# Loading the last 64 tokens of two batches in another order, and other transfer times for the planner of a sliding-window attention and two-matrix kernel

## The chip, the cores and the metric

The kernel runs on one core of a Trainium2 chip. The metric is the device time of one execution in microseconds (us).

## The reference

Attention with a window over 8 batches, 8 heads, 576 tokens and 64 numbers a head, then two matrix products with a leaky rectifier between them. Heads 0 to 3 see the last 32 tokens; heads 4 to 7 see every fourth of the last 128 ("dilated").

```
rel = pos[:, None] - pos[None, :]
mask_plain = (rel >= 0) & (rel < 32)
mask_dil = (rel >= 0) & (rel < 128) & (rel % 4 == 0)
attn = softmax(where(mask, q @ k.T / 8, -1e9))      # for each batch and head
x = (attn @ v), as [4608 tokens, 512]
h = x @ w_in                                        # [512, 2048]
out = max(0.01 * h, h) @ w_out                      # [2048, 512]
```

Inputs and output are float32. The kernel casts to float16 for TensorE.

## The kernel before

**Stages.** Batches 0 and 1 are "early" (`EARLY`): they are loaded in large runs of 1024 bytes (four tokens of a head), and q and k are turned by PE transposes through PSUM. Batches 2 to 7 are loaded in 128-byte pieces and turned by DVE. Each early batch is treated in two parts. Part 0 is its first 512 tokens, loaded by `load_group` in two groups of heads: group 1 (dilated) and group 0 (plain), each with q, k and v. Part 1 is "the rest", the last 64 tokens of all heads, loaded by `load_rest`: one load of q, one of k (128 KB each), one of v of the dilated heads (64 KB), and for batch 0 one of v of the plain heads (64 KB). `load_rest` casts q and k together on POOL (1024 numbers a partition), and the v loads in pieces of 512; for batch 0 it also runs a permutation of plain v on PE (`permute`).

`turn` brings q and k into the slots that the scores read. For part 1 it transposes the cast rest in eight PE transposes into the bank `tpb` and moves the result into `slots` by DVE copies (`move`, line 644). `unit` then does, for a pair of heads and a third of the tokens: scores on PE (line 854, for small dilated units 840, with a bias by line 837), the exponential on ACT (860), values and sums on PE (898, 892, 886), logarithm and exponential on ACT (930, 932), and the norm on DVE into `xt` (936). `xt` is the input of the up products.

The 4608 tokens are twelve chunks of 384 tokens, three for each pair of batches: chunk 0 is the first 384 tokens of batch 0, chunk 1 those of batch 1, chunk 2 the remaining tokens of both. `up` multiplies a chunk with a block of w_in (line 1091), and ACT applies the rectifier (1102). An up product needs all four row blocks of w_in, and all norms of its chunk. `down` (1275) and, later, `group` (1364) multiply with w_out. The last three chunks use `up_fast` (1188). w_in and w_out come in eight loads of 512 KB each (`load_w`), and each is cast to float16 in two pieces on POOL or DVE (line 272).

**The order of the work** is made by a planner, `_Plan.run`, when the kernel is built. Each task has an engine, an estimated duration, its dependencies and a priority (a lower number goes first). The planner simulates the engines and writes each engine's instructions in the order of their simulated starts; the chip runs each queue in that order, and waits are put in from the data's dependencies. A DMA is simulated as one server after another: its service is `took(n, size)` for n packets of `size` bytes, `AHEAD` says how many us of service may be queued when SP issues the next one, and `LATE` (or 0.8, or 0) us are added to the landing by the load's place. So these constants change no instruction, only the orders. From `LOCK` (60 us) on, the planner also lets POOL and DVE wait for each other on certain operations.

The first loads go in the order of the string `FIRST`, one letter a step, each with the next priority. Before, `b` and `c` are q and k of batches 0 and 1 (the first time for the dilated group, the second for the plain one), `v` and `y` their v, `i` a load of w_in, `o` a load of w_out, and `0` and `1` the rest of batches 0 and 1. `CON` places a load of constants among them. `RANKS` gives the priorities of the early batches' parts: batch 0 part 0 begins at 10 with steps of 6, its part 1 at 10 with steps of 0.5.

Where the plan leaves PE idle, a matmul on zeros is put in (line 1595). It has no use but to keep PE at work, and it waits for nothing.

Of the kernel before, what the change touches and what calls it, by code (L numbers as in the profile page):

```python
# [12 lines left out]
ALU = mybir.AluOpType  # L13

WIN = 32
AHEAD, LATE = 5.0, 4.0
WHEN = (-5.0, 15.0, 46.0, 70.0, 100.0, 126.0, 160.0, 188.0)
CON = -1484.5
LOCK = 60.0
AFTER = -1495.0  # L20
FIRST = "bvbviiii0iiiicoocoyoooooy1"
RANKS = ((10.0, 6.0), (10.0, 0.5), (15.0, 2.0), (25.0, 2.0))


# [37 lines left out]
class _Plan:  # L62
# [21 lines left out]

    def run(self):
        free, waiting, lock = {}, {}, {}
        server = 0.0

        def enter(t):
            for eng, _ in t.choices:  # L90
                waiting.setdefault(eng, []).append(t)

        for t in self.tasks:
            for d in t.deps:
                d.users.append(t)
            t.left = len(t.deps)
            if t.left == 0:
                enter(t)
        order = []
        while len(order) < len(self.tasks):  # L100
            best = None
            for eng, cand in waiting.items():
                if not cand:
                    continue
                here = free.get(eng, 0.0)
                if eng == "SP":
                    here = max(here, server - AHEAD)
                could = [t for t in cand
                         if not self.better_elsewhere(t, eng, max(here, t.ready), free)]
                if not could:  # L110
                    continue
                at = max(here, min(t.ready for t in could))
                pick = min(((t.ready + t.soft > at + 1e-9, t.prio, t.n), t)
                           for t in could if t.ready <= at + 1e-9)
                if best is None or (at, pick[1].n) < best[:2]:
                    best = (at, pick[1].n, eng, pick[1])
            at, _, eng, t = best
            for e, _ in t.choices:
                waiting[e].remove(t)
            t.eng, t.start, t.dur = eng, at, dict(t.choices)[eng]  # L120
            if at > LOCK and eng == "POOL" and t.kind in ("cast", "M", "A", "move") or (
                    at > LOCK and eng == "DVE" and t.kind in ("M", "A", "T")):
                t.dur += max(0.0, lock.get("DVE" if eng == "POOL" else "POOL", 0.0) - at)
                lock[eng] = at + t.dur
            free[eng] = at + t.dur
            if t.service:
                begin = max(at + t.dur + 0.9, server)
                server = begin + t.service
                t.done = server + 1.1 + t.late
            else:  # L130
                t.done = at + t.dur + t.lat
            order.append(t)
            for u in t.users:
                u.ready = max(u.ready, t.done)
                u.left -= 1
                if u.left == 0:
                    enter(u)
        order.sort(key=lambda t: (t.start, t.n))
        return order
# [3 lines left out]
def kernel(  # L143
# [14 lines left out]
    B, H, S, D = q.shape  # L158
# [31 lines left out]
    def dram(t, off, *dims):  # L190
        return bass.AP(tensor=t.tensor, offset=t.offset + off, ap=[list(d) for d in dims])
# [58 lines left out]


    def took(n, size):
        for a, ta, b, tb in ((4, 9.0, 128, 15.0), (128, 15.0, 256, 19.0), (256, 19.0, 1024, 48.0),
                             (1024, 48.0, 2048, 85.0)):
            if size <= b:
                return n * (ta + (tb - ta) * (size - a) / (b - a)) / 16e3
        return n * size / 25.6 / 16e3

    def load(queue, dst, src, n, size, deps, prio, slow=1.0):
        eng = ENG[queue]  # L260
        return plan.dma(queue, 0.7 if size == 128 else 0.48, took(n, size) * slow, deps,
                        lambda e: eng.dma_start(dst, src), prio,
                        LATE if prio > -1500 + len(FIRST) else 0.8 if prio >= AFTER else 0.0)

    def cast(dst, src, n, deps, prio, engines=("POOL",)):
        cost = {"POOL": 0.05 + n * 0.00102, "DVE": 0.08 + n * 0.00056, "ACT": 0.06 + n * 0.00087}
# [234 lines left out]
    def load_rest(b, prio):  # L501


        _, r_old = ring("REST", 1, r_users := [])
        sn, s_old = ring("STG", NST, s_users := [])
        st, lo = stg[sn], []
        for o, src in ((0, q), (1, k)):
            lo.append(load("SP", at(st, 0, 128, o * 256, [1, 256]),
                           dram(src, b * H * HS + 512 * D, [HS, 8], [4 * D, 16], [1, 256]),
                           128, 1024, s_old, prio))  # L510
        c = cast(at(rest, 0, 128, 0, [128, 8], [D, 2], [1, D]),
                 at(st, 0, 128, 0, [D, 8], [0, 2], [1, D]), 1024, lo + r_old, prio)
        s_users.append(c)
        vs, v_old, v_users = v_late[b]
        spread = bass.AP(tensor=vs.tensor, offset=vs.offset + 1024,
                         ap=[[4 * vs.ap[0][0], 16], [256, 4], [1, 256]])
        lv = load("SP", spread,
                  dram(v, (b * H + 4) * HS + 512 * D, [4 * D, 16], [HS, 4], [1, 256]),
                  64, 1024, v_old + t_vr[:1], prio)
        last = []  # L520
        if b == 0:
            vz, z_old, z_users = v_late[b, 0]
            lz = load("SP", bass.AP(tensor=vz.tensor, offset=vz.offset + 1024,
                                    ap=[[4 * vz.ap[0][0], 16], [256, 4], [1, 256]]),
                      dram(v, 512 * D, [4 * D, 16], [HS, 4], [1, 256]), 64, 1024, z_old + t_vr[1:],
                      prio)
            c_z = [cast(turned[i][0:64, 0:512], vz[0:64, 1024 + 512 * i:1536 + 512 * i], 512, [lz],
                        prio + 20) for i in range(2)]
            z_users += c_z
            last = permute((4, 5), c_z, RANKS[1][0], True)  # L530
            done = [t for t, _ in permuted]
            for t in t_gap:
                t.deps.extend(done)
            rings["X"] = [done, done]
        for vi in (2, 3, 0, 1):
            vt, d_users = kept[b, vi]
            c_v = []
            if vi >= 2:
                c_v = [cast(at(vt, 0, 64, 0, [1024, 2], [128, 4], [1, D]),
                            at(vs, 0, 64, 1024 + (vi - 2) * 512, [256, 2], [D, 4], [1, D]), 512,  # L540
                            [lv] + d_users, prio + 30)]
                v_users += c_v
            c_v += last[vi:vi + 1] if vi < 2 else []
            visits[b, vi, 1] = rest, [c], r_users, vt, c_v + seen_ones[b, vi], d_users
# [3 lines left out]
    def load_w(n, prio):  # L548
# [10 lines left out]
        else:  # L559
            x = 1024 * (n - 8)  # L560
            src = dram(moe_w_out, 128 * x, [2 * DM, 128], [1, 1024])
            dst = w_out
        t = load("SP", st, src, 128, 4096, old, prio, 1.3 if n < 4 else 1.0)
        for i in range(2):
            c = cast(dst[:, x + 512 * i:x + 512 * i + 512], st[:, 512 * i:512 * i + 512], 512, [t],
                     29 if n < 2 else prio, ("POOL",) if 4 <= n < 8 else CENG)
# [91 lines left out]
    def turn(b, hp, part, prio):  # L658
# [59 lines left out]
        if part == 1:  # L718
# [8 lines left out]
            if two == 2 and hp % 2:  # L727
                new = pair_moves[b, hp ^ 1]
            else:
                new, busy = [], users + other[1] * (two == 2)  # L730
                for hh, h in enumerate(heads_of(b, hp)):
                    p0 = 64 * hh
                    for o, bk in ((0, qb), (1, kb)):
                        x, dims = 512 * o + 16 * h, [[128, 4], [1, 16]]
                        if dil:
                            c, to = (0, [[144, 4], [4, 16]]) if o else (hh * S + 128, [[144, 4], [1, 16]])
                        elif o:
                            c, to, dims = PAD + 512, [[4, 16], [1, 4]], [[1, 16], [128, 4]]
                        else:
                            c, to = hh * S + 488, [[24, 4], [1, 16]]  # L740
                        step = PAD + S if o else 2 * S
                        new.append(move(at(bk, p0, p0 + 64, c, [step, two], *to),
                                        at(tpb, p0, p0 + 64, x, [32, two], *dims), 64 * two,
                                        [tq] + zq + zk + (busy if dil and o else []), prio))
                pair_moves[b, hp] = new
            q_users += new
# [752 lines left out]
    for n, step in enumerate(FIRST):  # L1499
        seen = FIRST[:n].count(step)  # L1500
        if step in "io":
            load_w(seen + (8 if step == "o" else 0), tick())
        elif step in "bvcy":
            ranks["bvcy".index(step) // 2, 1 - seen, step in "vy"] = tick()
        else:
            ranks[int(step)] = tick()

# [145 lines left out]
```

## Time and profile before

| | us |
|---|---|
| median of 3 runs (lowest, highest) | 306.11 (305.94, 306.44) |
| profiled execution, device time | 306.29 |
| its span, first to last instruction | 304.5 |
| PE busy in the span | 294.4 |
| DVE, ACT, POOL busy | 231.0, 188.7, 132.3 |

The granted clock was 1.00. A line of the profile is named L with the line of the code. A wait is put down to the instruction or the load that ended last before it. PE's busy time contains the idle matmuls (L1489 at the start, L1595 later), and a matmul's end is modelled, so that a matmul that starts 0.16 us after another may be shown 0.3 us long. The 40 slices of the span are 7.61 us each. SP is the queue that issues nearly all loads and stores; its rows show when a load is issued and not when it lands. The DMA engines moved 51.09 MB, and in the first 44 us they were busy nearly all the time.

### The profile page before, as it was taken

The numbers are of one execution on the slowest core, as the hardware profiler recorded it, in microseconds if no ns is written. First come the engines' busy times: TensorE is split into PE (matmuls) and PEld (weight loads), VectorE is DVE, ScalarE is ACT, GpSimd is POOL, SyncE is SP. The second block draws the span as 40 slices with busy tenths as digits, with TensorE's granted clock in tenths as the row PEclk, the third lists the DMA queues.
The fourth block names the chain that finished last, engine by engine and source line by source line (L and its number), as shares of the span: only waits on it lengthen the run. The fifth ranks groups of instructions, "written<-read, shape, count | busy, mean of one in ns | idle before, by whom it ended". The sixth has DMA issues, their size and how long they took to land.

```text
span 304.5 us, 7869 instructions
## 1 busy us (share of the span) xinstructions
PE 294.4 (97%) x2970; PEld 225.4 (74%) x2970; DVE 231.0 (76%) x478; ACT 188.7 (62%) x458; POOL 132.3 (43%) x179
## 2 busy tenths in 40 slices
PE   6889999999999999997999999999999999999994
PEld 3646655667777676786777777887788999999984
DVE  6875875689686869959888779879775899697552
ACT  3857854795556678464766567456565688767230
POOL 5469555393674949159094668665000000000000
PEclk9999999999999999999999999999999999999999
DMA  7999999999999899976999969793102110031124
GB/s 241 404 370 392 407 289 201 239 201 167 253 171 196 190 188 196 174 180 134 183 161 221 204 136 194 159 208 80 37 2 72 34 37 2 11 91 32 32 76 146
DMA packets 160390, 51.09 MB, mean 168 GB/s; under 512 B 137632, under 2 KB 157024, under 8 KB 160352
## 3 DMA queue, kind: packets, MB, share of 16 engines
q1 hardware_dynamic: 159520, 49.86, 68.3%
q10 hardware_dynamic: 832, 0.73, 0.8%
q8 instruction: 23, 0.38, 0.5%
q14 instruction: 15, 0.12, 0.1%
HBM read 41.13 MB, written 9.44 MB: 166 GB/s over the span
## 4 chain that ended last, share of the span: by engine, by line
PE 90%; DVE 5%; ACT 3%; DMA 1%; issue 1%; DVEq 0%
PE hps L1091 29%; PE fps L1364 26%; PE fps L1275 9%; PE ops L1015 3%; PE hps L1188 3%; PE ops L1188 3%; PE ops L1063 2%; PE sps L1188 2%; PE tp L1188 1%; PE tp L692 1%; PE ops L1364 1%; PE tp L982 1%; PE sps L982 1%; DVE ee L1008 1%; PE fps L347 1%; PE tp L975 1%
## 5 line engine op out<-in xcount | busy, mean ns | idle before, releaser
L1091 PE MATMUL hps<-xt,w_in 128*128 128x384 f16 (+1 forms) x640 | 111.7, 310 | 0.8 <-DVE w_in L272 0.6
L1102 ACT ACTIVATE gt<-hps 128x384 f16<-128x384 f32 (+1 forms) x160 | 72.8, 461 | 43.8 <-PE hps L1091 41.5
L1091 PEld LDWEIGHTS <-w_in 128*128 128x128 f16 x640 | 56.7, 98 | 26.3 <-DVE w_in L272 1.0
L1364 PEld LDWEIGHTS <-gt 128*128 128x128 f16 x672 | 64.4, 98 | 9.7
L679 POOL COPY slots<-turned 64x576 f16<-64x576 f16 x48 | 36.3, 757 | 47.4 <-DVE turned L674 45.5
L1364 PE MATMUL fps<-w_out,gt 128*128 128x256 f16 x416 | 53.6, 273 | 0.0
L272 POOL CAST nat<-stg 128x576 f16<-128x576 f32 (+1 forms) x53 | 43.0, 834 | 9.7 <-DMA stg<-in_q_dram 3.5
L1275 PE MATMUL fps<-w_out,gt 128*128 128x512 f16 x128 | 32.4, 379 | 0.0
L1037 DVE TENSOR_TENSOR rc<-ops,recs 96x384 f16<-96x384 f32 x48 | 25.7, 538 | 0.3
L1393 ACT COPY stg<-fps 128x512 f32<-128x512 f32 (+1 forms) x24 | 12.8, 532 | 14.4 <-PE fps L1364 14.4
L1008 DVE TENSOR_TENSOR ee<-ee,con 128x576 f16<-128x576 f16 x24 | 17.2, 722 | 3.5 <-ACT ee L994 3.5
L1033 DVE RECIPROCAL recs<-ops 96x6 f32<-96x6 f32 x48 | 8.7, 181 | 14.7 <-PE ops L1015 12.5
L1401 DVE TENSOR_TENSOR osb<-fps,stg 128x512 f32<-128x512 f32 x18 | 12.4, 687 | 9.7 <-PE fps L1364 5.6
L272 POOL CAST vd<-v_all 128x1024 f16<-128x1024 f32 (+2 forms) x20 | 18.0, 918 | 2.7 <-DMA v_all<-in_v_dram 2.7
L1211 ACT ACTIVATE gt<-stg 128x384 f16<-128x384 f32 x36 | 18.0, 524 | 1.1 <-DVE stg L1205 1.1
L1275 PEld LDWEIGHTS <-gt 128*128 128x128 f16 x128 | 11.6, 98 | 9.1
L644 DVE COPY slots<-tp 64x128 f16<-64x128 f16 (+7 forms) x42 | 13.4, 333 | 6.3 <-PE tp L692 5.6
L674 DVE STREAM_TRANSPOSE turned<-nat 128x576 f16<-128x576 f16 x24 | 17.7, 751 | 0.0
L685 DVE STREAM_TRANSPOSE slots<-nat 128x576 f16<-128x576 f16 x24 | 17.7, 745 | 0.0
L1008 DVE TENSOR_TENSOR el<-el,con 128x576 f16<-128x576 f16 x24 | 15.0, 630 | 2.7 <-ACT el L994 2.5
L1188 PEld LDWEIGHTS <-w_in 128*128 128x128 f16 x192 | 16.4, 98 | 0.5 <-DVE w_in L1119 0.3
L994 ACT ACTIVATE ee<-sps 128x288 f16<-128x288 f32 x24 | 9.8, 409 | 8.4 <-PE sps L982 5.8
(158 smaller groups left out, 529.3 us busy)
## 6 DMA issues: line engine op xcount, KB each, us to landing
stg<-in_q_dram SPq DMA_DIRECT2D x48, 144.0 KB, 3.2
stg<-in_k_dram SPq DMA_DIRECT2D x48, 144.0 KB, 2.9
v_all<-in_v_dram SPq DMA_DIRECT2D x24, 256.0 KB, 3.8
v_all<-in_v_dram SPq DMA_DIRECT2D x24, 192.0 KB, 3.2
gt<-in_moe_w_in_dram SPq DMA_DIRECT2D x5, 512.0 KB, 7.1
out_dram<-osb SPq DMA_DIRECT2D x22, 96.0 KB, 2.0
out_dram<-osb SPq DMA_DIRECT2D x40, 48.0 KB, 1.8
out_dram<-osb SPq DMA_DIRECT2D x25, 64.0 KB, 2.2
```

What stands on the lines that cost most here:

```text
L272: ENG[e].tensor_copy(out=dst, in_=src)
L674: lambda e: nc.vector.transpose(xb, na[:, 0:S]), prio)
L679: lambda e, p0=p0, hh=hh: nc.gpsimd.tensor_copy(out=at(qb, p0, p0 + 64, hh * S + o, *od), in_=at(xb, p0, p0 + 64, i, *id_)), prio, 0.0, "m ...
L685: lambda e: nc.vector.transpose(kb[:, PAD:PAD + S], na[:, S:2 * S]), prio)
L1008: nc.vector.tensor_tensor(out=x, in0=x, in1=mk, op=ALU.mult)
L1037: nc.vector.tensor_tensor(out=at(xb, 0, 96, 768 * n + 64 * i, [256, 3], [128, 2], [1, D]), in0=at(ot, 0, 96, 0, [130, 3], [65, 2], [1, D]) ...
L1091: nc.tensor.matmul(ht[:, 0:n], at(w_in, 0, 128, i * DFF + j // 2 * 256 + j % 2, [2, 128]), at(xt[m % 2], 0, 128, i * 1152 + x0, *dims), st ...
L1102: lambda e: nc.scalar.activation(out=gt[c % NG][:, j * n_c + x:j * n_c + x + n], in_=ht[:, 0:n], func=AF.Prelu, alpha=0.01),
L1188: nc.tensor.matmul(cell[:, n * z:n * z + n], lhs(2 * p + z, i), rhs(i), start=first and z == 0 and i == 0, stop=z == 1 and i == 1, skip_gr ...
L1211: lambda e: nc.scalar.activation(out=at(g, 0, 128, j * n_c + n * y, [n_c, 2], [1, n]), in_=at(src, 0, 128, 0, [n, 2], [1, n]), func=AF.Pre ...
L1275: nc.tensor.matmul(ft, g[:, j * n_c + tt * 128:j * n_c + tt * 128 + 128], w_out[:, j * DM:j * DM + DM], start=(j == 0), stop=(j == NJ - 1))
L1364: nc.tensor.matmul(bk[:, x:x + HN], tl[:, off + j * step:off + j * step + 128], rhs(j), start=first and x == 0 and j == 0, stop=j == HJ - ...
```

## The change

1. In `load_rest`, the source of the rest's q and k is read with the 16 groups of four tokens outermost and the 8 heads inside, instead of the heads outermost. A partition of the stage holds 8 x group + head instead of 16 x head + group. In `turn`, the eight moves of the rest read the transposed bank in steps of 8 elements instead of 1.
2. `FIRST` gets a table, `LOADS`, which gives each letter its batch, group and kind. In the string, `0` goes from behind the fourth load of w_in to before the first. The rest of the order is the same under new letters.
3. The planner counts at most eight transfers in flight for SP (`FLIGHT`) up to 60 us, `LATE` goes from 4.0 to 2.5 and the first loads' 0.8 to 0.3, `took` gets other figures for packets of 128 to 2048 bytes, and the factor of 1.3 on the first four loads of w_in goes.

```diff
-AHEAD, LATE = 5.0, 4.0
+AHEAD, LATE = 5.0, 2.5
...
+FLIGHT = 8
 AFTER = -1495.0
-FIRST = "bvbviiii0iiiicoocoyoooooy1"
+FIRST = "bvaw0iiiiiiiicooeoyooooox1"
+LOADS = {"b": (0, 1, False), "v": (0, 1, True), "a": (0, 0, False), "w": (0, 0, True),
+         "c": (1, 1, False), "y": (1, 1, True), "e": (1, 0, False), "x": (1, 0, True)}
...
-        server = 0.0
+        server, lands = 0.0, [0.0] * FLIGHT
...
                 if eng == "SP":
-                    here = max(here, server - AHEAD)
+                    here = max(here, server - AHEAD, lands[-FLIGHT] if here < LOCK else 0.0)
...
                 t.done = server + 1.1 + t.late
+                lands.append(server + 1.1)
...
-        for a, ta, b, tb in ((4, 9.0, 128, 15.0), (128, 15.0, 256, 19.0), (256, 19.0, 1024, 48.0),
-                             (1024, 48.0, 2048, 85.0)):
+        for a, ta, b, tb in ((4, 9.0, 128, 13.3), (128, 13.3, 256, 18.3), (256, 18.3, 1024, 48.5),
+                             (1024, 48.5, 2048, 95.0)):
...
-                        LATE if prio > -1500 + len(FIRST) else 0.8 if prio >= AFTER else 0.0)
+                        LATE if prio > -1500 + len(FIRST) else 0.3 if prio >= AFTER else 0.0)
...
-                           dram(src, b * H * HS + 512 * D, [HS, 8], [4 * D, 16], [1, 256]),
+                           dram(src, b * H * HS + 512 * D, [4 * D, 16], [HS, 8], [1, 256]),
...
-        t = load("SP", st, src, 128, 4096, old, prio, 1.3 if n < 4 else 1.0)
+        t = load("SP", st, src, 128, 4096, old, prio)
...
-                        x, dims = 512 * o + 16 * h, [[128, 4], [1, 16]]
+                        x, dims = 512 * o + h, [[128, 4], [8, 16]]
...
-                            c, to, dims = PAD + 512, [[4, 16], [1, 4]], [[1, 16], [128, 4]]
+                            c, to, dims = PAD + 512, [[4, 16], [1, 4]], [[8, 16], [128, 4]]
...
-                                        at(tpb, p0, p0 + 64, x, [32, two], *dims), 64 * two,
+                                        at(tpb, p0, p0 + 64, x, [2, two], *dims), 64 * two,
...
-        elif step in "bvcy":
-            ranks["bvcy".index(step) // 2, 1 - seen, step in "vy"] = tick()
+        elif step in LOADS:
+            ranks[LOADS[step]] = tick()
```

## The prediction

> **What bounds the kernel now.** I read the busy table and its forty slices first, then PE's waits, then PE's timeline where it waits, then SP's issues and the DMA rate by window, last POOL's waits and DVE's timeline in the middle. The profiled execution took 306.29 us, of which 304.5 us is the span and 1.79 us lies around it; the median of the runs is 306.11 us, 0.18 us less. All sums below are made on 306.29 and brought to the median at the end. A difference of 0.2% (0.61 us) is about the least that a measurement of this kernel can tell from none.
>
> ```profile
> PE 294.4 (97%) x2970; PEld 225.4 (74%) x2970; DVE 231.0 (76%) x478; ACT 188.7 (62%) x458; POOL 132.3 (43%) x179
> PE   6889999999999999997999999999999999999994
> ```
>
> PE is the bound. Its row is at 9 from the fourth slice (22.8 us) on, but for one 7 at 137 to 145 us and the end. So only the first 22 us and that one dip hold anything to gain. PE's waits in the whole trace, longest first (line, what it waited for, us in total, times, longest):
>
> ```profile
> PE ops L1015 <- DVE ee L1008: 1.6, 1, 1.6
> ...
> PE hps L1091 <- DVE w_in L272: 0.6, 1, 0.6
> ```
>
> The dip is one wait of 1.6 us. The early waits are short, because the program fills planned waits with idle matmuls (L1595). They count as busy, so the timeline has to be read by line (start, length, engine and line):
>
> ```profile
> 16.82 0.61 PE L1595 MATMUL fps<-warm 128*128 128x512 f16 x2
> 17.71 0.28 PE L898 MATMUL ops<-ee,vp 128*64 128x96 f16 x4 [0.29 <-DVE xt L936]
> 17.80 0.28 PE L886 MATMUL ops<-ee,ones 128*64 128x192 f16 x2
> 18.00 1.25 PE L1595 MATMUL fps<-warm 128*128 128x512 f16 x5
> 19.09 1.16 PE L1091 MATMUL hps<-xt,w_in 128*128 128x384 f16 x6
> 20.89 0.50 PE L1091 MATMUL hps<-xt,w_in 128*128 128x384 f16 x2 [0.64 <-DVE w_in L272]
> 21.22 0.38 PE L1595 MATMUL fps<-warm 128*128 128x512 f16 x1
> 21.80 1.46 PE L1091 MATMUL hps<-xt,w_in 128*128 128x384 f16 x8 [0.20 <-ACT gt L1102]
> ```
>
> From 16.82 to 21.80 us, 4.98 us, PE does eight up matmuls (1.30 us, as the eight from 21.80 to 23.10 show) and one group of values (0.29 us, 17.71 to 18.00). **The hole is 4.98 - 1.30 - 0.29 = 3.39 us.** It is bounded by the last norms of batch 0's first part (DVE, to 19.2 us) and by the fourth w_in block: it landed at 18.90 us, and its cast on DVE (19.67, 1.16 us where the same cast took 0.41 elsewhere) ended at 20.83.
>
> The loads, by window (length, clock, DMA busy share, GB/s), and then SP's issues (start, length of issuing):
>
> ```profile
> 14.00:16.00 2.00, 1.00 1.01 414
> 16.00:17.00 1.00, 1.00 1.04 344
> 17.00:18.00 1.00, 1.00 1.12 290
> 18.00:19.00 1.00, 1.00 1.06 325
> ```
>
> ```profile
> 9.46 0.79 SPq L262 DMA_DIRECT2D stg<-in_q_dram  x1
> ...
> 13.45 2.88 SPq L262 DMA_DIRECT2D gt<-in_moe_w_in_dram  x3
> 18.92 0.33 SPq L262 DMA_DIRECT2D xt<-in_moe_w_in_dram  x1
> ```
>
> The DMA engines are full, yet the rate falls while the rest of batch 0 (the loads issued at 9.46 to 12.8) passes. SP issues with eight loads in flight: the w_in load of 13.45 goes out when the load eight before it has landed (13.43), that of 18.92 after the landing at 18.90.
>
> **The change, part by part.**
>
> *Token groups outermost.* Each of the rest's q and k loads shows eight engines' completions in the trace (q 17.55 to 18.07, k 18.50 to 19.04), a w_in load sixteen; of the next w_in load eight engines finish at 18.99 to 19.66 and eight at 20.18 to 20.55. So half of the engines carried both loads: 2 x 128 packets over 8 is 32 packets of 46 ns (the row's own 1024-byte packets), 1.47 us; over 16 it would be 0.74 us. The windows agree: 3 x 414 - (344 + 290 + 325) = 283 KB lost, 0.68 us. Loads behind it come 0.7 us sooner. PE has no wait for a load from 22 to 54 us, so alone this is worth nothing there; it is what lets PE run ahead. The Trainium skill ("DMA: Bandwidth & Descriptors", how many engines, in the section on why a DMA increments its semaphore by 16) says that a DMA uses the largest count up to 16 that divides the slowest dimension of both sides, which gives 8 for 8 heads and 16 for 16 token groups; by it the spread is sure, by the rows alone it is likely. The second such load (batch 1, landed by 46.7, used at 51.20) gains as much and is waited for by nobody.
>
> *The stride of the eight moves.* They read PSUM in steps of 8 elements where they read runs. The rows have 216 to 228 ns for runs (425 to 449 where held) and 272 to 289 for those with a step of 128: at most 0.06 us x 6, 0.36 us of DVE per batch, at least nothing. I take 0.2, on DVE alone.
>
> *The rest ahead of w_in.* Four issues (0.79 + 0.62 + 0.61 + 0.57 = 2.6 us of SP) go before eight. The first w_in issue moves from 6.38 to about 9.4 us; the batch's own loads keep the engines busy until 12.17, which hides it. The 384 KB put w_in back by 384/414 = 0.93 us: the fourth block, 1.28 us behind the third (15.99), would land at 15.99 + 1.28 + 0.93 = 18.2. In the trace one engine ran 1.25 us behind the fifteen others there (17.65 to 18.90; a 16 KB instruction packet of 1.04 us lies at 16 us), so 18.2 to 19.4, against 18.90. The rest would have landed by about 13.2 instead of 19.5.
>
> On POOL the rest's cast (1.04 us) and two of 0.80 and 0.61 go between w_in casts; POOL has gaps of 0.65 to 1.84 us there. On DVE eight moves (2.07 us at 23.75) come in front of the last norms and casts. They need the transpose bank, whose last users end at 15.6, so they run at about 16.5 to 18.6. DVE is idle for 5.00 - 4.35 = 0.65 us in 17 to 22 and 0.37 in 13 to 17, so norms and casts could slip by up to 1.05 us; w_in casts going to POOL instead (0.61 each) can make it nothing. The cast held to 1.16 us stood against the rest's cast on POOL (19.51 to 20.55); that goes, worth up to 0.75 us, and can recur earlier. Ups began in effect at 21.22 - 1.30 = 19.92; I expect 19.3 to 20.9 and take +0.2 us. A rule speaks against this move: the Trainium skill ("SBUF — State Buffer", who interferes with whom) lets DVE and GpSimd block each other for a whole instruction on a shared port pair. By it the 0.75 us is moved, not saved, and the sum would be 0.75 us longer; the 1.16 us cast agrees with it.
>
> What fills the hole: the rest's PE work now lies behind it. Eight transposes 0.45 (23.10 to 23.55); four score groups 0.34 + 0.33 + 0.34 + 0.34; four value groups 0.33 + 0.33 + 0.29 + 0.29; permutations 1.52 (26.48 to 28.00): 4.56 us for a hole of 3.39. Least: the transposes, 0.45. Most: 3.39. Each unit runs scores, exponential, values, so transposes, two or three score groups and a pair of value groups are likely: 0.45 + 1.0 + 0.4, about **1.8 us taken out of PE's later path**.
>
> *Is 1.8 us kept?* At 53.77 the down products of chunk 0 are used up and chunk 1 needs the last norm of batch 1 (DVE, 53.69). Its last v landed at 44.87, was cast by 46.44, and its values ran at 48.29 to 51.75 between downs. Those downs moved forward leave the units nearer to each other; some 2 us of slack, enough for 1.8.
>
> *Planner's figures (transfer times, eight in flight, 2.5 for 4.0 us of lateness).* No instruction is added; the orders of all queues are made anew. With 1.5 us less margin a cast can stand at the head of POOL before its load. POOL's waits from 60 to 210 us, and a line of DVE's timeline:
>
> ```profile
> POOL slots L679 <- DVE turned L674: 45.5, 14, 7.3
> POOL nat L272 <- DMA stg<-in_k_dram: 2.4, 2, 2.0
> POOL nat L272 <- DMA stg<-in_q_dram: 1.1, 1, 1.1
> ```
>
> ```profile
> 139.54 2.95 DVE L1008 TENSOR_TENSOR ee<-ee,con 128x576 f16<-128x576 f16 x1
> ```
>
> POOL waits 3.8 us for loads (0.3 in a row not shown) and 45.5 for DVE: room enough, and none of the four waits for loads reached PE. The one stall that did is the mask of 139.54, held for 2.95 us (0.40 free) beside a row of POOL casts. A new order can drop it (-1.6), keep it, or make more (+1.6 each). I take +0.3, since the order before shows so few.
>
> **Sum:** 306.29 - 1.8 + 0.2 + 0.3 = 305.0 us, less 0.18: **304.8 us**.
>
> **Rivals.**
>
> *More of it:* the hole is filled to the brim (-3.39) and the 1.6 us stall goes: 306.1 - 5.0 = 301.1; half of it 302.8. For it: 4.56 us of work is at hand. Against: the chain within a unit. 0.16.
>
> *Given back at 54 us:* the units of batch 1 keep their place and PE waits there: 306.1. For: its v comes only 0.7 us sooner. Against: values 2 us behind their cast. 0.10.
>
> *Still eight engines:* w_in and all behind come 0.7 us later than I say; half shows: 305.2. Nothing in the rows speaks for it. 0.07.
>
> *Slower:* the new order between 60 and 200 us sets POOL's casts against DVE's masks more often, with PE's values queued behind, 1.6 us each as at 139.54. One more is 306.4, within the measure; it decides from two more on: 304.8 + 3.2 = 308.0. For: some twenty DVE and POOL instructions there run over 0.5 us longer than the shortest of their line and shape, and only one stall of over a microsecond comes of them, which an arbitrary new order may not repeat. Against: the planner models this lock. 0.23.
>
> **Numbers.** Forecast 0.44, 303.6 to 305.4. Faster 0.44 + 0.16 + 0.06 = 0.66, same 0.11, slower 0.23. The range takes half of the first rival and the slower case with one to two stalls: 302.6 to 307.3.
>
> **What would show it.** Right: L1595 rows after 16 us gone or few, rest transposes on PE before 18 us, sixteen completions of the rest loads, no rate below 380 GB/s from 16 to 19 us, ups in full from about 20 us. Wrong: PE waits for DVE or w_in before 22 us as long as now, a PE wait at 50 to 54 us for batch 1, or more than one wait of over 1 us after 60 us.

## The result and the profile after

The changed kernel takes **313.3 us** (median of 4 runs, 312.3 to 314.0) against 306.1 us beside it: ratio 1.0231, 95% interval 1.0210 to 1.0252. It is slower by 7.2 us; the forecast of 304.8 and the whole range, to 307.3, lie below it. Measured again (e1) it took 311.2 us, ratio 1.0159 (1.0142 to 1.0176). The two intervals don't meet; what differs is told at e1. A few runs lie more than 1.5% above the fastest of their kernel: the ratios leave them out, some medians do not, so the ratios are what I go by.

The profiled execution took 314.0 us, its span 312.2 us. The busy table and PE's row of forty slices (7.8 us each):

```profile
PE 296.9 (95%) x2963; PEld 226.4 (73%) x2963; DVE 230.7 (74%) x478; ACT 188.7 (60%) x459; POOL 128.5 (41%) x178
...
PE   6889999999999989999996999989999999999995
```

The row of before had one weak slice after 23 us. Here there are three: the fifteenth (109 to 117 us), the twenty-second (164 to 172) and the twenty-seventh (203 to 211). PE's waits in the whole trace of after, longest first (lines stand four further down than before, so L1019 is the values line that was L1015):

```profile
PE ops L1019 <- DVE ee L1012: 3.4, 3, 1.3
PE tp L696 <- POOL nat L276: 2.3, 1, 2.3
PE sps L979 <- POOL slots L683: 2.1, 1, 2.1
```

PE waits for masks (DVE) three times, for a copy by POOL once, and once, at 5.9 us, for POOL's cast of a first load. POOL's and DVE's waits from 60 to 210 us, the window that the prediction showed:

```profile
POOL nat L276 <- DMA stg<-in_q_dram: 19.7, 7, 8.8
POOL slots L683 <- DVE turned L678: 19.4, 11, 3.5
POOL nat L276 <- DMA stg<-in_k_dram: 9.0, 3, 3.1
POOL nat L276 <- DMA v_all<-in_v_dram: 2.3, 1, 2.3
```

```profile
DVE slots L689 <- POOL nat L276: 6.1, 2, 3.1
DVE turned L678 <- POOL nat L276: 0.6, 1, 0.6
```

Before, POOL waited 3.8 us for loads there, and DVE not once for POOL. Now POOL waits over 30 us for loads, and DVE 6.7 us for POOL. The casts stand at the head of POOL before their data.

To see where PE loses time I use one sum for all kernels: the time elapsed less the columns that PE's useful matmuls have streamed by then (2.4 columns a nanosecond, the 0.16 us from start to start of 384 columns). Idle matmuls count as lost, and so does half of every stretch in which PE works at half its clock.

| PE time lost, us, by | 30 us | 42 us | 100 us | 139 us | 220 us | the end | span |
|---|---|---|---|---|---|---|---|
| before | 12.4 | 12.7 | 14.5 | 16.1 | 20.1 | 22.5 | 304.5 |
| after | 13.9 | 14.3 | 16.9 | 19.6 | 27.8 | 30.3 | 312.2 |
| after, second time (e1) | 13.1 | 13.4 | 16.0 | 18.7 | 24.6 | 26.9 | 308.8 |
| new order and layout, old figures (e4) | 11.0 | 11.9 | 14.0 | 15.8 | 18.2 | 20.5 | 302.4 |
| e4 with less lateness (e7) | 10.5 | 11.5 | 13.6 | 14.5 | 16.9 | 19.1 | 301.0 |
| after with shorter late loads (e17) | 13.6 | 13.6 | 16.3 | 19.9 | 22.2 | 24.5 | 306.3 |

The differences at the end are those of the spans within 0.3 us, so the table is the whole account. After loses 1.5 us more than before by 30 us, and 5.2 us more between 100 and 220 us (10.9 against 5.6).

### The profile page after: what moved, and what is told of

The parts are those of the page before. It is cut to its first block, busy times and chain, and to the rows that moved or that the text cites. A ratio compares the mean times of both kernels' runs of the same rounds, so it can differ in the third digit from the quotient of the medians.

```text
span 312.2 us, 7855 instructions
## 1 busy us (share of the span) xinstructions
PE 296.9 (95%) x2963; PEld 226.4 (73%) x2963; DVE 230.7 (74%) x478; ACT 188.7 (60%) x459; POOL 128.5 (41%) x178
## 4 chain that ended last, share of the span: by engine, by line
PE 77%; DVE 7%; DMA 6%; SPq 3%; issue 2%; ACT 2%; POOL 2%; POOLq 0%; DVEq 0%
PE hps L1095 25%; PE fps L1368 22%; PE fps L1279 7%; DMA stg<-in_q_dram 4%; SPq L266 3%; PE hps L1192 3%; PE ops L1192 3%; PE ops L1019 3%; DMA v_all<-in_v_dram 2%; DVE slots L648 2%; PE sps L1192 2%; PE ops L1067 2%; PE tp L1192 1%; PE ops L1368 1%; POOL nat L276 1%
## 5 line engine op out<-in xcount | busy, mean ns | idle before, releaser
L1095 PEld LDWEIGHTS <-w_in 128*128 128x128 f16 x640 | 57.3, 98 | 25.7 <-issue 1.3
L276 POOL CAST nat<-stg 128x576 f16<-128x576 f32 (+1 forms) x53 | 39.8, 775 | 40.6 <-DMA stg<-in_q_dram 25.2
L683 POOL COPY slots<-turned 64x576 f16<-64x576 f16 x48 | 37.3, 776 | 22.4 <-DVE turned L678 19.4
L1041 DVE TENSOR_TENSOR rc<-ops,recs 96x384 f16<-96x384 f32 x48 | 25.7, 541 | 0.2
L276 POOL CAST vd<-v_all 128x1024 f16<-128x1024 f32 (+2 forms) x20 | 18.9, 960 | 4.9 <-DMA v_all<-in_v_dram 3.9
L1279 PEld LDWEIGHTS <-gt 128*128 128x128 f16 x128 | 11.5, 98 | 9.1
L940 DVE TENSOR_TENSOR xt<-ops,rc 128x192 f16<-128x192 f32 (+1 forms) x26 | 8.9, 348 | 9.0 <-ACT rc L936 8.8
```

The costliest lines, as they stand in the source:

```text
L276: ENG[e].tensor_copy(out=dst, in_=src)
L683: lambda e, p0=p0, hh=hh: nc.gpsimd.tensor_copy(out=at(qb, p0, p0 + 64, hh * S + o, *od), in_=at(xb, p0, p0 + 64, i, *id_)), prio, 0.0, "m ...
L1041: nc.vector.tensor_tensor(out=at(xb, 0, 96, 768 * n + 64 * i, [256, 3], [128, 2], [1, D]), in0=at(ot, 0, 96, 0, [130, 3], [65, 2], [1, D]) ...
L1095: nc.tensor.matmul(ht[:, 0:n], at(w_in, 0, 128, i * DFF + j // 2 * 256 + j % 2, [2, 128]), at(xt[m % 2], 0, 128, i * 1152 + x0, *dims), st ...
L1279: nc.tensor.matmul(ft, g[:, j * n_c + tt * 128:j * n_c + tt * 128 + 128], w_out[:, j * DM:j * DM + DM], start=(j == 0), stop=(j == NJ - 1))
```

## The experiments

**e1. The change again, unaltered**, on the chip of e2 to e4.

> The changed kernel once more, unaltered, for a second profile. All theories: 312 to 314 us. If the one engine that lagged by 2.1 us at 5 to 8 us in the first profile was chance, the PE wait of 2.3 us at 8.5 us is gone and the span is 1 to 2 us shorter; if it belongs to the change, it stands there again. The waits of PE at 110, 165 to 168 and 207 us (1.4, 3.3 and 1.5 us) must recur if they come from the order.

Measured: 311.17 us (310.57 to 311.54), ratio 1.0159 (1.0142 to 1.0176). PE's waits:

```profile
PE ops L1019 <- DVE ee L1012: 4.2, 2, 3.0
PE ops L902 <- DVE xt L940: 1.2, 1, 1.2
```

The gap at 5.9 us is not there. The stalls at 109 and 202 us recur (1.2 and 3.0 us); at 165 us, where after waited for 0.9 and 2.1 us in a row, e1 waits for 0.3 us, although every engine's instructions stand in the same order. So not all three of the late stalls belong to the order alone.

What e1 has early in place of the gap is a stretch at half the clock. PE's windows, first in e1, then in e4, which is told below (length, busy time of PE, PEld, DVE, ACT and POOL, clock, DMA share, GB/s):

```profile
23.40:26.80 3.40, 3.40 (x21) 1.44 (x20) 1.20 (x6) 1.84 (x5) 3.40 (x7) 0.50 1.09 397
```

```profile
23.40:26.80 3.40, 3.40 (x34) 1.82 (x32) 1.23 (x5) 2.97 (x8) 3.40 (x7) 1.00 1.06 391
```

PE is busy all through in both, but in e1 its granted clock is 0.50 (the number third from the end). By PE time lost, e1 loses 1.6 us in this stretch and e4 0.2: 1.4 of the 2.1 us by which e1 is behind e4 at 30 us.

The longest of the late stalls, 3.0 us, can be followed back queue by queue. SP, POOL, DVE and PE in the timeline of e1 (start, length, what it did, and in brackets the idle time before it):

```profile
183.56 9.85 SPq L266 DMA_DIRECT2D out_dram<-osb  x14
193.45 1.06 SPq L266 DMA_DIRECT2D stg<-in_q_dram  x2
194.56 4.65 SPq L266 DMA_DIRECT2D stg<-in_k_dram  x4
```

```profile
197.43 1.27 POOL L276 CAST nat<-stg 128x576 f16<-128x576 f32 x2 [8.45 <-DMA stg<-in_q_dram]
201.37 1.28 POOL L276 CAST nat<-stg 128x576 f16<-128x576 f32 x2 [2.67 <-DMA stg<-in_k_dram]
```

```profile
198.12 0.78 DVE L678 STREAM_TRANSPOSE turned<-nat 128x576 f16<-128x576 f16 x1 [2.66 <-POOL nat L276]
...
202.07 0.78 DVE L689 STREAM_TRANSPOSE slots<-nat 128x576 f16<-128x576 f16 x1 [3.09 <-POOL nat L276]
...
204.56 0.88 DVE L1012 TENSOR_TENSOR ee<-ee,con 128x576 f16<-128x576 f16 x1
```

```profile
201.02 1.46 PE L1095 MATMUL hps<-xt,w_in 128*128 128x384 f16 x8
205.49 0.36 PE L1019 MATMUL ops<-vp,ee 128*128 128x65 f16 x6 [3.01 <-DVE ee L1012]
```

The last two loads of a q go out only after fourteen stores, 9.85 us of issuing. The q lands, and POOL, which has stood at its cast for 8.45 us, casts at 197.43. DVE has stood at the turn of that tile for 2.66 us. The k behind it repeats this: POOL waits 2.67 us, DVE 3.09. The mask at 204.56 needs none of these tiles; ACT had written what it reads by 200.29. It only stands behind those turns on DVE, and PE's values stand behind the mask. The stall is handed down three in-order queues.

**e2. After with the old lateness.**

```diff
-AHEAD, LATE = 5.0, 2.5
+AHEAD, LATE = 5.0, 4.0
```

> The changed kernel with LATE back at 4.0 and nothing else. Margin theory (loads planned 1.5 us earlier make POOL stand before its loads, 34 us of such waits against 4 before, and PE's values wait behind): POOL's waits for loads after 60 us fall below 10 us, the three mid stalls go, 307.5 to 309.5 us. Early theory (the rest ahead of w_in costs the time): unchanged, 312 to 314. Lottery theory (any new order loses the few stalls of the old one): anything from 306 to 313, with stalls at other places.

Measured: ratio 1.0038 (1.0006 to 1.0069), median 308.71. By the ratios 1.2%, some 3.7 us, of e1's loss goes, but not for the reason given: POOL's waits for loads did not fall below 10 us, they rose (19.3 us for q and 14.3 for k). One stall of 4.3 us on PE came at 170 us, for a copy by POOL. So what the old lateness gives back is not a shorter wait of POOL for its loads; what it is stays open.

**e3. Before with the planner's figures alone** (lateness, transfer times, eight in flight, 0.3, no 1.3; old order, old layout).

> The kernel before with the planner's figures alone (transfer times, eight in flight, 2.5 and 0.3 of lateness, no factor of 1.3); the loads, their order of the first 26 steps and the layout of the rest as before. Margin theory: 309.5 to 312 us with POOL waiting over 20 us for loads after 60 us. Early theory: 305.5 to 306.5. Lottery theory: 306.5 to 312, in no relation to POOL's waits for loads.

Measured: 307.52 us, ratio 1.0050 (1.0023 to 1.0078). The figures cost 1.5 us on the old order.

**e4. Before with the new layout and order alone** (parts 1 and 2 of the change; old figures).

> The kernel before with the new layout of the rest and the rest ahead of w_in, the planner's figures as before. My forecast's theory of the hole: 304 to 305.5 us. Early theory: 308 to 312, ups starting at 23 us or later. Margin theory: at most 306.5. Lottery theory: 306.5 to 311 with mid stalls although POOL waits under 10 us for loads.

Measured: **304.48 us** (304.03 to 304.81), ratio 0.9941 (0.9924 to 0.9958). PE in e4, from where before has its hole (lines here stand two further down than before):

```profile
15.95 0.62 PE L694 MATMUL tp<-con,rest 128*128 128x128 f16 x8
...
16.79 1.05 PE L349 MATMUL fps<-pair,el 128*128 128x256 f16 x8
17.77 0.62 PE L355 MATMUL fps<-turned,el 64*128 64x128 f16 x8
...
20.12 0.50 PE L1597 MATMUL fps<-warm 128*128 128x512 f16 x2
...
22.60 1.46 PE L1093 MATMUL hps<-xt,w_in 128*128 128x384 f16 x8
```

The rest's transposes and the permutation stand where idle matmuls stood, and only one row of idle matmuls of 0.50 us and one of 0.28 (at 22.15) are left. DMA in e4 by window (length, clock, share, GB/s):

```profile
16.00:17.00 1.00, 1.00 1.04 410
17.00:18.00 1.00, 1.00 1.01 393
18.00:19.00 1.00, 1.00 1.02 410
```

The dip to 290 GB/s is gone. After 22 us PE has no stall over 0.5 us, and the wait of 1.6 us at 140 us is not there: no mask from 136 to 143 us takes over 1.03 us, where before had one of 2.95. DVE in e4:

```profile
139.03 0.95 DVE L1010 TENSOR_TENSOR ee<-ee,con 128x576 f16<-128x576 f16 x1
```

So parts 1 and 2 reach the time that was forecast, and the loss is in part 3. Where e4's gain lies is another matter, told below.

**e5. After with the old transfer times** (all four figures of `took` back to 15, 19, 48 and 85).

> The changed kernel with the old transfer times in the planner (15, 19, 48 and 85 in place of 13.3, 18.3, 48.5 and 95); eight in flight, 2.5 and 0.3 of lateness stay. Transfer-time theory (with 13.3 the planner counts on loads that the chip brings later, up to 10 us late at 180 us; with 15 they come before the plan): 304 to 306 us, loads at 140 to 200 us within 2 us of the plan or before it. Lateness theory (2.5 for 4.0): 307.5 to 310. Lottery theory: 304 to 311, loads against the plan of no account.

Measured: 304.9 us, ratio 0.9977 (0.9946 to 1.0007). With the old transfer times some 6 us of e1's 311.2 are gone.

**e6. e4 with the new transfer times**, all four, nothing else.

> The kernel before with the new layout and the rest ahead of w_in (304.5 us) and the new transfer times alone. Transfer-time theory: 307.5 to 311, loads 4 to 10 us behind the plan at 140 to 200 us, runs spread over 3 us or more. Lateness theory: 304 to 305. Lottery theory: 304 to 311.

Measured: 310.7 us (309.37 to 311.65), ratio 1.0142 (1.0104 to 1.0179): 6.2 us on top of e4. PE's longest wait is of the kind that after has, a slot that POOL copies late:

```profile
PE sps L977 <- POOL slots L681: 2.1, 1, 2.1
```

**e7. e4 with the lateness of 2.5 alone.**

> The kernel before with the new layout and the rest ahead of w_in (304.5 us) and LATE at 2.5 alone. Transfer-time theory: 304 to 306, since with the old transfer times the loads come before the plan and 1.5 us less of margin is not used. Lateness theory: 307 to 309.5. Lottery theory: 304 to 311.

Measured: **303.59 us** (302.85 to 304.88), ratio 0.9917 (0.9889 to 0.9946), span 301.0. No loss. It is the lowest time of the study and beats both kernels; its interval overlaps those of e4, e9 and e10.

So the transfer times carry the loss, with the full change (e5) and without the rest of it (e6). Next, which of the four.

**e8. After with the 128-byte figure alone back at 15.0.**

> The changed kernel with the one figure for packets of 128 bytes back at 15.0 and all else as changed. Transfer-time theory in its narrow form (the 128-byte loads of batches 2 to 7, 48 q and 48 k loads, are what runs late): 304 to 306.5. If the longer stores or the figures of other sizes matter: 308 to 311. Lottery theory: 304 to 311.

Measured: 307.11 us, ratio 1.0026 (1.0002 to 1.0050). About 4 us of e1's loss go with this one figure.

**e9. The order without the layout** (part 2 alone).

> The kernel before with the rest ahead of w_in alone: heads outermost again, moves without a stride. The instructions stand in the same order on every engine as in the run with both (304.5 us), so the difference is the spread over the engines alone. Spread theory (eight engines carry 0.7 us more, w_in and all loads behind come 0.7 us later, and PE now waits for w_in): eight completions for each of the rest's loads, the fourth w_in block 0.7 us later, 304.9 to 305.3 us. Order theory (the place in the queue is all): 304.3 to 304.7. Lottery theory says nothing on it.

Measured: 303.93 us (303.32 to 305.58), ratio 0.9940 (0.9918 to 0.9962), the same as e4. The instructions of every engine stand in the order of e4, so this is the layout alone. The rest's q and k show eight completions each where e4's q shows sixteen, and the third and fourth w_in loads land at 19.17 and 20.44 us instead of 18.47 and 19.76: 0.7 us later, as the prediction sized it. And it is worth nothing, which is also what the prediction said.

**e10. e4 with the 128-byte figure alone at 13.3.**

> The kernel before with the new layout and the rest ahead of w_in (304.5 us) and 13.3 in place of 15.0 for packets of 128 bytes alone. Transfer-time theory in its narrow form: 307.5 to 310.5, PE waits at 160 to 210 us behind casts that wait for loads. If the other figures (stores of 2048 bytes at 95) carry as much: 305.5 to 308. Lottery theory: 304 to 311.

Measured: 304.11 us (303.0 to 305.03), ratio 0.9937 (0.9913 to 0.9961). No loss at all: the figure that took 4 us off in e8 adds nothing here. The narrow theory, that late q and k loads reckoned too short are enough by themselves, falls.

**e11. e7 with the 128-byte figure at 16.7**, above the old one.

> The kernel before with the new layout, the rest ahead of w_in, LATE at 2.5 (303.6 us) and 16.7 in place of 15.0 for packets of 128 bytes: as far from the old figure as 13.3 on the other side. Transfer-time theory (a planner that counts on late loads loses nothing, one that counts on early loads does): 303 to 305, no PE wait over 1 us after 60 us. Lottery theory (any step away from 15 costs the same): 306 to 311.

Measured: 308.13 us (307.09 to 308.88), ratio 1.0069 (1.0052 to 1.0085), 4.5 us more than e7. More margin in the figure did not help. PE's longest wait:

```profile
PE ops L1065 <- DVE rc L1039: 1.4, 1, 1.4
```

DVE never waits for POOL here and SP issues earlier than planned, so this is a loss of another kind: PE waits for DVE at 116 to 117.5 us, and from 118.5 to 122 us its clock is at half. From 100 to 122 us e11 loses 4.3 us of PE time, e7 0.6. A figure moves more than the margin; it re-draws the order.

**e12. e4 with the first figures alone** (eight in flight, 0.3, no 1.3).

> The kernel before with the new layout and the rest ahead of w_in (304.5 us), with eight in flight, 0.3 in place of 0.8 and without the factor of 1.3; transfer times and LATE as before. These act on the first 60 us. If they take back the early gain (the changed kernel had 13.1 us of PE time lost by 30 us against 11.0 in the run without planner figures): 305 to 306.5 with 12 us or more lost by 30 us. If the transfer times did that too: 304 to 305.

Measured: 304.72 us, ratio 0.9964 (0.9946 to 0.9981). Harmless.

**e13 and e14. e4 with the 128- and 256-byte figures (13.3, 18.3), and with the 1024- and 2048-byte ones (48.5, 95).**

> The kernel before with the new layout and the rest ahead of w_in (304.5 us) and the load figures alone: 13.3 for 128 bytes and 18.3 for 256 bytes; 1024 and 2048 bytes as before. The four figures together gave 310.7, 13.3 alone 304.1. If the cause lies in the load figures taken together: 308 to 311. If it lies in the figures of 1024 and 2048 bytes (stores, v): 303.5 to 305.5.

> The same base (304.5 us) with 48.5 for 1024 bytes and 95 for 2048 bytes alone. If the cause lies in these: 308 to 311, with DVE waiting for POOL after 60 us. If it lies in the load figures: 303.5 to 305.5. If both this and its counterpart stay near 304.5, only the sum of the figures does it (lottery theory in its strict form: no figure has a price of its own).

Measured: e13 313.1 us, ratio 1.0183 (1.0115 to 1.0252); e14 306.93 us, ratio 1.0029 (1.0007 to 1.0051). 13.3 alone adds nothing to e4 and 13.3 with 18.3 adds over 2%; 48.5 with 95 adds some 2.5 us. The two pairs together (e6, 1.0142) cost no more than e13 alone. No figure has a price of its own.

**e15 and e16. After with longer issues reckoned for SP, and after with more lateness.** In every order that had lost over 1% so far, SP was late against the planner's own starts. Either figure should make the planner expect that.

```diff
-        return plan.dma(queue, 0.7 if size == 128 else 0.48, took(n, size) * slow, deps,
+        return plan.dma(queue, 0.8 if size == 128 else 0.6, took(n, size) * slow, deps,
```

```diff
-AHEAD, LATE = 5.0, 2.5
+AHEAD, LATE = 5.0, 7.0
```

> The changed kernel with the planner's cost of issuing a transfer on SP raised from 0.70 to 0.80 us for 128-byte loads and from 0.48 to 0.60 for the others, about what SP's rows show from one issue to the next; all else as changed. Drift theory (SP falls behind the plan, loads stand behind stores, a cast heads POOL's queue before its load has landed, a turn heads DVE's queue before the cast, masks and PE's values stand behind it): 304 to 306.5, DVE waits for POOL under 2 us. Lottery theory: 304 to 311.

> The changed kernel with LATE at 7.0, so that the casts and turns are planned 4.5 us later behind their loads. Drift theory: DVE's waits for POOL after 60 us go from 7.3 us to under 2, 304 to 306.5 us; with 4.0 it was 4.3 us of such waits and 308.7. Lottery theory: 304 to 311.

Measured: e15 311.73 us, ratio 1.0217 (1.0148 to 1.0286); e16 313.05 us, ratio 1.0256 (1.0202 to 1.0310). Both expectations were wrong. Both orders are new, and the lateness did not go: DVE waits for POOL 13.5 us in e15 and 8.2 in e16 (60 to 215 us).

**e17. The orders of after, with shorter late loads.** The loads of q and k of batches 2 to 7 move 24 of their 36 runs a partition; the rest of the computation runs on what else is in the stage. Every engine's instructions stand in the order of after, so that this takes away lateness and nothing else.

```diff
-                lo = [load("SP", at(st, 32 * a, 32 * a + 32, 0, [32, 36], [1, 32]),
-                           dram(src, base + (a // 2) * 2 * HS + (a % 2) * 32,
-                                [D, 32], [32 * D, 36], [1, 32]),
+                lo = [load("SP", at(st, 32 * a, 32 * a + 32, 384, [32, 24], [1, 32]),
+                           dram(src, base + 384 * D + (a // 2) * 2 * HS + (a % 2) * 32,
+                                [D, 32], [32 * D, 24], [1, 32]),
```

> The changed kernel, the instructions of all engines in the same order, but each 128-byte load of q and k of batches 2 to 7 moves 24 of its 36 runs (a third of q and k is left out). The plan is untouched; only the DMA engines have less to move. If the loss comes from loads that the chip brings later than the plan says, in a stretch where the DMA engines are full (their share is 0.92 to 1.09 from 44 to 140 us): POOL's waits for loads after 60 us fall from 23 us to under 8, DVE's for POOL from 7 to under 2, 304 to 306.5 us. If the order of the instructions itself costs the time (lottery theory, loads of no account): 309.5 to 312.

Measured: median 307.73 us, ratio 1.0038 (1.0010 to 1.0066), against 1.0159 for e1: 1.2%, some 3.5 us. Part of this is PE's clock. All of e1's runs have a mean granted clock of 0.987 to 0.994. Of e17's runs, four at 0.998 or more took 305.3 to 306.0 us, the others, at 0.994 or less, 307.2 us and more. Between runs of either kernel at 0.992 to 0.994 the difference is some 2.8 us (medians of 310.9 and 308.1). DMA from 44 to 140 us, first in e1, then in e17 (length, clock, share, GB/s at the end of the row after the engines' busy times):

```profile
44.00:140.00 96.00, 94.44 (x941) 66.02 (x939) 77.40 (x152) 61.04 (x159) 61.24 (x76) 1.00 0.98 196
```

```profile
44.00:140.00 96.00, 93.48 (x928) 65.00 (x927) 77.14 (x149) 61.15 (x158) 61.61 (x77) 1.00 0.82 176
```

The DMA engines have room, DVE's waits for POOL from 60 to 210 us go from 7.3 us to none, and e1's stall of 3.0 us at 202 us is gone. One stays:

```profile
PE ops L1019 <- DVE ee L1012: 2.2, 1, 2.2
```

It is at 109 us, and its cause is not a load. DVE and POOL there, in e17:

```profile
107.77 3.75 DVE L1012 TENSOR_TENSOR ee<-ee,con 128x576 f16<-128x576 f16 x1
```

```profile
107.97 1.28 POOL L276 CAST nat<-stg 128x576 f16<-128x576 f32 x2
109.19 2.02 POOL L276 CAST vd<-v_all 128x1024 f16<-128x1024 f32 x2
```

The mask takes 3.75 us where a free one takes 0.40, beside four POOL casts in a row that last until 111.21. The same mask took 2.77 us in e1, and PE waited for 1.2 us there. The Trainium skill ("SBUF — State Buffer", who interferes with whom) says that a DVE instruction with both inputs in SBUF contends with a GpSimd instruction that reads SBUF. The mask is one of that kind, and the trace agrees; that one mask can be held by a whole row of casts is what this trace adds. The early part (13.6 us lost by 30 us) also stays as it was in after.

**e18. e4's orders with heavier loads**, the counterpart: one of each four late q and k loads in runs of 64 bytes instead of 128.

```diff
-                lo = [load("SP", at(st, 32 * a, 32 * a + 32, 0, [32, 36], [1, 32]),
+                lo = [load("SP", at(st, 32 * a, 32 * a + 32, 0, [32, 36], [16, 2], [1, 16]) if a == 0
+                           else at(st, 32 * a, 32 * a + 32, 0, [32, 36], [1, 32]),
...
```

> The kernel before with the new layout and the rest ahead of w_in (304.5 us), the instructions in the same order, but one of the four loads of each q and k of batches 2 to 7 goes in 64-byte runs instead of 128: the same bytes in a quarter more packets. The plan is untouched, the DMA engines have more to do. If late loads make the loss: POOL waits for loads and DVE for POOL as in the changed kernel, 307.5 to 312 us. If the order itself does: 304 to 305.5.

Measured: 304.11 us (303.66 to 304.72), ratio 0.9932 (0.9915 to 0.9949). It says nothing on lateness, since the stress did not come about: the DMA share from 44 to 140 us is 0.95 (e4: 0.94), and the loads are not later.

## Why the prediction was wrong, step by step

**The hole of 3.39 us and what fills it: right by 30 us, with both terms too small.** I took 1.8 us out of PE's later path and 0.2 us of later ups, 1.6 together; e4 is 1.4 us ahead of before by 30 us. But the ups are later by much more than 0.2: before, they began in effect at 19.92, in e4 they begin at 22.60, some 2.7 us later. So the rest's work done ahead of them is 1.4 + 2.7 = 4.1 us of the 4.56 at hand. What came late is on record: the fourth block of w_in landed at 19.76 us, not by 18.2 to 19.4, and on DVE, behind the eight moves and a held cast, the last cast of w_in ended at 22.25 and the last norm before the ups at 22.51. I had let them slip by up to 1.05 us.

**"Is 1.8 us kept?": no, in e4.** Its lead on before falls from 1.4 us by 30 us to 0.75 by 42 us, 0.5 by 100 and 0.25 by 139. The first half goes at 38.7 to 40 us, and not at 54 us as my rival "given back" had it: there the last units of batch 1's first part leave PE an idle matmul row of 0.49 us (38.69 to 39.11) and a wait for a slot that DVE copies. What brings e4 to 2.0 us at the end of the span, and to 1.65 in the medians, is the mask of 140 us, which the new order dropped: from 139 to 143 us before loses 1.8 us and e4 0.1. That is half of my first rival ("the 1.6 us stall goes"). So the forecast's time came out in e4 with another make-up. In e7 both are there: it is 1.5 us ahead of before at 139 us, and 3.1 at 143.

**The cast that could recur: right as a risk.** I weighed that the hold of 0.75 us goes or moves. In e4 the second cast of w_in on DVE takes 1.32 us, from 19.85, where a free one takes 0.41. It moved, and nothing was saved.

**The stride of the moves: right.** Eight moves took 2.34 us in e4 against my 2.07 + 0.2.

**The layout: right.** 0.7 us of landing, nothing in time (e9).

**The planner's figures, "I take +0.3": the step that failed.** It measured +6.7 us (e1 311.2 less e4 304.5). On the old order the same figures cost 1.5 us (e3), so the price is that of the figures and the new order together. By PE time lost (e1 less e4) that is 2.1 us by 30 us and 4.3 us between 100 and 220. My reason was POOL's idle time: "POOL waits 3.8 us for loads and 45.5 for DVE: room enough". Idle time is not room when a queue is in order. What stood at the head of POOL was a cast without its data, behind it copies that DVE and PE needed, and on DVE the turn of that tile ahead of masks for other batches. How long POOL waits does not decide either: in e4 it waits 23 us for loads and DVE only 3.1 us for POOL, and PE does not stall. It matters once the wait is handed to DVE with a mask behind it.

**"A new order can drop it, keep it, or make more (+1.6 each)".** I priced held masks, and one is in the loss: the one at 109 us, 1.2 us in e1 and 2.2 in e17. But the larger part had no term at all: loads later than planned, and PE's clock, which went to half for 3.4 us behind some of the waits (told in the last section). I looked at lateness as 1.5 us less margin for one cast; the transfer times, which place every later load too, from 44 to 140 us in a stretch where the DMA engines are 0.94 to 0.98 busy, I didn't price apart from it.

**The slower rival, "new order … sets POOL's casts against DVE's masks" (308.0, 0.23): the right side and part of the mechanism.** Its time was too small, and the range ended with it.

**Signs.** From 16 to 19 us no rate below 380 GB/s, sixteen completions, idle matmuls few: all seen. "More than one wait of over 1 us after 60 us" was named as the sign of being wrong, and it came. Ups "in full from about 20 us" came at 22.6 in e4, at 25.7 in after.

**What is shown, and what stays open.** Shown: the loss lies in the figures, above all in the transfer times, when they meet the new order (e3, e4, e5, e6); with the same orders, some 3 us of it go when the late loads are shorter, and DVE's waits for POOL with them (e17). Only seen together: the planner's simulated start of each load can be set against its issue in the trace. For loads planned at 100 to 120 us, SP is on average 4.4 to 7.8 us behind in after, e1, e2, e6, e13, e15 and e16 (ratios from 1.0038 to 1.0256) and at most 3.1 us in the others, none above 1.0069. The two groups overlap: e2 is 7.7 us behind at 1.0038. Open: why these sums of figures give these orders and their parts don't (e10, e13, e14), and why two ways to plan for later loads did not help (e15, e16). Of the early part, 2.1 to 2.9 us against e4 by 30 us, most is accounted for: in after 2.4 us are the gap told below with its half clock, in e1 1.4 us are the stretch at half clock alone. The first figures alone don't make it (e12, 10.8 lost). Open is what makes the clock fall in these runs and not in e4.

## What to carry to other kernels

A change to a planner's constants, though it changes no instruction, re-makes every order: here the new figures took 2.2% (e1 against e4), and no constant had a price that could be added to another's, so each set has to be run as a whole. That the old figures were a margin which held the order together is not shown: more margin lost time as well (e11, e16). When an order is re-made, an engine's idle share does not tell what will wait: look at what stands at the head of each in-order queue, what it waits for, and who stands behind it two queues on. When PE stalls, look at its clock behind the stall too: here that added up to 1.7 us to waits of 1.2 us and more. And split a change by its parts first: the order gave 0.6%, with less lateness 0.8% (e7), and the bundle hid both.

## What the runs showed of the hardware

In after one of the sixteen DMA engines fell behind at 5 to 8 us: the sixteenth completion of a first q load came at 7.79 us, the fifteenth at 5.74. e17, with the same orders, showed such a lag again (a first k load, 8.77 against 6.94 us; PE waited for 1.3 us until 9.3, and its clock was 0.50 from 11.4 to 14.8), e1 did not. What makes it is open. PE was busy for 0.43 us in that gap, and then ran at half speed. PE's windows of after (length, busy time of PE, PEld, DVE, ACT and POOL, clock, DMA share, GB/s):

```profile
5.80:8.50 2.70, 0.43 (x5) 0.10 (x2) 0.75 (x2) 0.58 (x1) 0.61 (x1) 0.95 1.04 356
8.50:11.90 3.40, 3.39 (x19) 2.30 (x19) 1.88 (x5) 1.45 (x3) 1.17 (x2) 0.53 1.07 374
11.90:13.00 1.10, 1.10 (x21) 0.84 (x19) 0.49 (x2) 0.90 (x4) 0.00 (x0) 1.00 0.91 236
```

The third number from the end is the granted clock: 0.53 for the 3.4 us after the gap, which by 3.4 x 0.47 costs up to 1.6 us more than the gap itself. The Trainium skill ("TensorE: Matmul & The Clock Gate", part 1) puts the return to half rate behind an idle window of about 3.4 us; the half rate and the 3.4 us until it ends agree, but here 2.3 us of waiting were enough.

Such stretches are part of the loss all through this case. Ahead of 300 us, before, e3, e4, e7 to e10, e12, e14 and e18 have none in their traces. After has two (8.3 to 11.7 and 168.7 to 172.1 us), e1, e2, e5, e6, e11, e16 and e17 have one each of 3.4 us, e13 and e15 one each of 6.8 us. Where PE has work, 3.4 us at half its clock cost up to 1.7 us. Each begins within a PE wait of 1.2 us or more, or at most 2.2 us behind one. But e1's wait of 3.0 us at 202 us has none behind it, nor has e17's of 2.2 us at 109 us. What decides is open.

The 64-byte runs in a quarter of the late q and k loads cost no measurable time (e18: 0.9932 against 0.9941).
